# Issuing the small SBUF-to-SBUF transfers from ACT instead of SP, with the order of the work planned anew

## The chip, the cores and the metric

The kernel runs on one core of a Trainium2 chip. The metric is the device time of one execution in microseconds (us). Five engines work in parallel and each takes its own instructions in order: PE (matrix multiply; PEld is its weight load), DVE (vector), ACT (scalar and activation), POOL (GpSimd) and SP, which in this kernel only issues transfers. ACT can issue transfers too. A transfer is issued on the queue of the engine that issues it and then carried by the core's DMA engines.

## What is computed

A linear attention with a decaying state, and behind it two feed-forward networks over the same 3072 tokens (384 columns, 2048 hidden), all in float32:

```python
# B, H, S, D = 4, 8, 768, 48; for each batch and head, over the time t
cur = einsum('bhd,bhe->bhde', u * k_t, v_t)
y_t = einsum('bhd,bhde->bhe', r_t, state + cur)
state = w_t[..., None] * state + einsum('bhd,bhe->bhde', k_t, v_t)
...
x = y.transpose(0, 2, 1, 3).reshape(B * S, H * D)
h = x @ w_in                                   # first network
x = (maximum(h, 0) + alpha * minimum(h, 0)) @ w_out
h = x @ w_in2                                  # second network
out = (h * clip(h + 3, 0, 6) / 6) @ w_out2
```

## The kernel before

**Attention.** The 3072 tokens are cut into 12 thirds of 256 tokens, and the 8 heads into 4 pairs, so there are 48 units (third t, pair pr; number n = 4t + pr). `add_third` loads and weighs the tokens of a third (`load_v`, `load_rk`, `weigh_tokens` L375, `red` L382). `add_unit` does a unit: it loads it (`load`, L412), makes two scans on DVE (L430, L444), scales (L465, DVE or POOL), multiplies on PE (L519, L527, L565, L569, L644, L651, L655), and on ACT it builds diagonals (L502, four instructions), sums a check (L490), copies (L558, L441) and scales states (L589). Its output is split into two float32r parts, hi (ACT, L680) and lo (DVE, L686).

**The transfers of this change.** The columns of the networks' input lie on 128 partitions in three blocks. Pairs 0 to 2 write their parts straight into `XT[j]` (tile names xt, rows 0 to 111 of a block). Pair 3 has no block of its own: its parts go into a staging tile `x3` (name x in the trace, one buffer), and six small transfers (`spread`, L696; 32 KB each, two heads by three blocks) carry them into the free 16-row gaps of the three blocks. So each third has one group of six, 12 groups and 72 transfers in all. A group waits for all hi and lo parts of its third (`before`), and slot 0 of a token block j waits for both groups of its two thirds (`xt_ops`).

**Networks.** The tokens stand in 6 blocks of 512; each network goes over 6 blocks by 16 hidden chunks, which makes 192 slots. A slot (`add_slot`) is nine matmuls into h, `pq` on ACT (L908 or L910), `gate` on DVE (L915 or L919), `ghi` on ACT (L925), `glo` on DVE or POOL (L928), and nine matmuls into acc; each product is three float32r matmuls (L871 to L873). Weights arrive packed (`add_weights`: load L825, then ACT L95, DVE L98 and L103, ACT L839, DVE or POOL L843). Block 0 needs thirds 0 and 1 (units 0 to 7), so the first matmul of slot 0 is the end of a prologue; until then the plan fills PE's gaps with dummy matmuls (`warm`, L772). The units of the other thirds run beside the slots of the first network. The first network's outputs go to memory by SP (`store`, L985) and come back for the second.

**The order.** Nothing is ordered by hand. `Plan.op` records every piece with its possible engines, its modelled duration, a due time in slots and its dependences; `Plan.run` simulates all engines and always takes the earliest piece that can start, the one with the lowest due first. The result is each engine's program order. `URGENCY` shifts due times by kind and stage (below -0.5 slots, to 16, to 80, to 95), and may pin a kind to an engine. SP is modelled as a queue with an issue time (`ISSUE`) and a flight time (`FLIGHT`). `SPARE` is added to the due time of a piece that could run elsewhere when it stands for DVE.

Of the kernel before, what the change touches and what calls it, by code (L numbers as in the profile page):

```python
# [109 lines left out]
def weight_range(nc, v, raw):  # L110
# [8 lines left out]
    "add_range.upper": {3: (2.5, None)},  # L119
    "add_slot.glo": {1: (0, "DVE"), 2: (0, "DVE")},  # L120
    "add_slot.h_": {1: (-3.0, None), 2: (1.0, None), 3: (-1.0, None)},
    "add_third.load_v": {0: (-6.0, None)},
    "add_third.red": {1: (0.5, None), 2: (-1.5, None)},
    "add_unit.add_output.lo_": {0: (1.0, None)},
    "add_unit.diag": {1: (4.0, None)},
    "add_unit.kt": {0: (-3.0, None), 2: (-3.0, None)},
    "add_unit.load": {1: (-1.5, None)},
    "add_unit.recip": {0: (-4.0, None)},
    "add_unit.scan_g": {0: (-4.0, None), 1: (-1.0, None)},
    "add_unit.scan_t": {1: (-1.0, None)},  # L130
    "add_unit.triangle": {0: (2.0, None)},
    "add_weights.hi": {0: (-2.0, None)},
    "add_weights.lo": {1: (-1.5, None)},
    "add_weights.load": {0: (1.0, None), 1: (-2.5, None)},
    "add_weights.rest": {1: (-2.0, None)},
    "join": {0: (-7.0, None)},
    "negate": {0: (-5.0, None)},
    "scale_half": {0: (0, "POOL")},
    "second": {2: (-0.5, None), 3: (2.0, None)},
    "state1": {1: (7.5, None)},  # L140
    "weigh_tokens": {0: (0, "POOL"), 1: (1.0, "DVE"), 2: (0, "DVE")},
# [3 lines left out]
class Plan:  # L145
# [8 lines left out]
    ISSUE, FLIGHT = 0.45, 1.6  # L154
    SPARE = 0
# [15 lines left out]
    def op(self, where, due, fn, after=(), new=(), use=(), pair=False, kind=None):  # L171

        kind = kind or fn.__qualname__.replace("<locals>.", "").split(".", 1)[1]
        if due < self.STAGES[-1]:
# [3 lines left out]
            if engine and len(where) > 1:  # L178
                where = {engine: where[engine]}
        o = {"where": where, "due": due, "fn": fn, "id": len(self.ops), "out": []}  # L180
        o["kind"] = kind
# [17 lines left out]
    def run(self):  # L199
# [6 lines left out]
        free = {e: self.BEGIN[e] for e in ready}  # L206
# [19 lines left out]
        pair = queue = 0.0  # L226
# [8 lines left out]
        while True:  # L235
# [11 lines left out]
            t, _, e, o = best  # L247
# [3 lines left out]
            o["eng"], o["start"], o["end"] = e, t, t + d  # L251
# [3 lines left out]
            if e == "SP":  # L255
                queue = o["end"] = max(t + self.ISSUE + self.FLIGHT, queue) + d
                free[e] = max(t + self.ISSUE, queue - self.FLIGHT - d)
# [14 lines left out]
def fast_path(es, tc, unit, tok, vch, ub, w1, w2, alpha, out, flag, alp, x2d):  # L272
    nc = tc.nc
# [80 lines left out]
    def add_third(t):  # L354
# [7 lines left out]
        v_op[t] = plan.op({"SP": 1.26}, due + 2, load_v, new=[vb]), vb  # L362
        pb = plan.buf("p", 2)
        reds = []
        for c in range(2):
# [22 lines left out]
            o = plan.op({"SP": 1.26}, due + c, load_rk, new=[rb])  # L388
# [9 lines left out]
    def add_unit(n):  # L398
# [15 lines left out]
        o_load = plan.op({"SP": 1.3}, d - 4 if n else -50.0, load, new=[ub_])  # L414
# [247 lines left out]
        def add_output(o_pc, yb2):  # L662
# [30 lines left out]
            if pr == 3:  # L693

                def spread(e, h, i):
                    nc.sync.dma_start(  # L696
                        XT[j][48 + 64 * h : 64 + 64 * h, i, :, cs].bitcast(F32),
                        u["x3"][64 * h + 16 * i : 64 * h + 16 * i + 16].bitcast(F32),
                    )

                before = list(ops)
                for h in range(2):
                    for i in range(NK):
                        ops.append(
                            plan.op(
                                {"SP": 0.48}, d + 2.6, lambda e, h=h, i=i: spread(e, h, i),
                                before, use=[xt_buf[j], x3b],
                                kind="spread",
                            )
                        )  # L710
# [98 lines left out]
    def add_weights(keys, due):  # L809
# [38 lines left out]
        o_l = plan.op({"SP": 1.26 * n}, due - 4, load, new=[wb])  # L848
# [473 lines left out]
```

## Time and profile before

| | us |
|---|---|
| median of 3 runs | 937.88 (932.49 to 1141.69) |
| the profiled execution | 939.31 |
| its span, first to last instruction | 937.5 |
| PE busy | 919.5 (98%) |
| DVE busy | 553.0 (59%) |
| ACT busy | 528.8 (56%) |
| POOL busy | 139.2 (15%) |

The span is taken from the profile; 1.8 us of the execution's time lie around it. A matmul's busy time includes its way through the array and overlaps with its neighbours, so PE can look busy while its matmuls start farther apart than they could. Instructions that issue transfers are not counted as busy time of their engine. Shares over the whole span mix a prologue, a stage in which the first network is fed while its weights are still being unpacked, and a long rest; the views by stretch keep them apart.

### The profile page before, as it was taken

What the parts mean: (1) busy time and instruction counts of PE and PEld (TensorE: products, weight loads), DVE (VectorE), ACT (ScalarE), POOL (GpSimd) and SP (SyncE); (2) the same over time, 40 slices, a digit from 0 to 9 for tenths busy, and PEclk for the clock granted to TensorE, in tenths of its full rate; (3) what the DMA queues carried; (4) which work ended last, traced back from release to release, by engine and by line L of the source; (5) the groups of instructions that cost most, each with busy time, mean ns of one, the idle gap of its engine ahead of it and who ended that gap; (6) DMA issues with size and microseconds to landing.
All of it is one profiled execution on the core that took longest, in us unless ns stands there. A gap on an engine that the chain in (4) does not pass through costs nothing.

```text
span 937.5 us, 13798 instructions
## 1 busy us (share of the span) xinstructions
PE 919.5 (98%) x4999; PEld 753.4 (80%) x4999; DVE 553.0 (59%) x957; ACT 528.8 (56%) x1260; POOL 139.2 (15%) x128
## 2 busy tenths in 40 slices
PE   8999998999999999999999999999999999999997
PEld 6876777888888888888888888888888888888885
DVE  7889996765756665564368987353353443443432
ACT  5988765655655655565357887363353443443331
POOL 7511021100100010010013254020020010200000
PEclk9999999999999999999999999999999999999998
DMA  8798223321322221110045540050140320400001
GB/s 274 227 266 275 68 84 103 110 72 56 119 65 74 98 59 41 56 54 6 8 135 203 176 161 1 0 202 1 48 155 0 135 68 1 168 34 1 35 1 37
DMA packets 36750, 86.20 MB, mean 92 GB/s; under 512 B 5056, under 2 KB 7488, under 8 KB 36672
## 3 DMA queue, kind: packets, MB, share of 16 engines
q1 hardware_dynamic: 36240, 84.44, 28.2%
q8 instruction: 41, 0.67, 0.3%
q10 hardware_dynamic: 432, 0.79, 0.2%
q14 instruction: 37, 0.30, 0.1%
HBM read 73.41 MB, written 9.44 MB: 88 GB/s over the span
## 4 chain that ended last, share of the span: by engine, by line
PE 90%; DVE 3%; DMA 2%; ACT 2%; issue 1%; POOL 0%; SPq 0%; ACTq 0%; DVEq 0%; POOLq 0%
PE acc L871 14%; PE h L871 14%; PE acc L872 14%; PE acc L873 14%; PE h L873 13%; PE h L872 13%; PE A L519 3%; PE y L651 2%; DMA un<-in_unit 2%; PE y L644 2%; PE A L527 1%; DMA rk<-in_tok 1%; DVE tg L444 1%; ACT wa L95 1%; PE y L655 1%
## 5 line engine op out<-in xcount | busy, mean ns | idle before, releaser
L871 PE MATMUL acc<-g,w 128*128 128x512 f32 x576 | 227.8, 396 | 0.0
L872 PE MATMUL acc<-g,w 128*128 128x512 f32 x576 | 225.0, 391 | 2.5 <-DVE g L928 2.5
L873 PE MATMUL acc<-g,w 128*128 128x512 f32 x576 | 224.6, 390 | 0.0
L925 ACT ACTIVATE g<-pg 128x512 fp32r<-128x512 f32 x192 | 120.9, 630 | 135.1 <-PE acc L873 85.8
L928 DVE TENSOR_TENSOR g<-pg,g 128x512 fp32r<-128x512 f32 x162 | 112.6, 696 | 116.5 <-ACT g L925 114.8
L872 PEld LDWEIGHTS acc<-g,w 128*128 128x128 f32 x576 | 108.3, 188 | 25.0 <-DVE g L928 4.0
L919 DVE SCALAR_TENSOR_TENSOR pg<-q,h 128x512 f32<-128x512 f32 x96 | 65.9, 686 | 105.4 <-ACT q L910 105.2
L871 PEld LDWEIGHTS acc<-g,w 128*128 128x128 f32 x576 | 108.8, 189 | 21.9 <-issue 0.4
L873 PEld LDWEIGHTS acc<-g,w 128*128 128x128 f32 x576 | 108.3, 188 | 22.4
L910 ACT ACTIVATE q<-h,three 128x512 f32<-128x512 f32 x96 | 65.6, 684 | 94.9 <-PE h L873 94.8
L871 PE MATMUL h<-xt,w 128*128 128x512 f32 x288 | 113.5, 394 | 2.1 <-DVE pg L915 2.0
L872 PE MATMUL h<-xt,w 128*128 128x512 f32 x288 | 112.6, 391 | 0.0
L873 PE MATMUL h<-xt,w 128*128 128x512 f32 x288 | 112.6, 391 | 0.0
L871 PE MATMUL h<-x,w 128*128 128x512 f32 x288 | 112.0, 389 | 0.0
L872 PE MATMUL h<-x,w 128*128 128x512 f32 x288 | 112.0, 389 | 0.0
L873 PE MATMUL h<-x,w 128*128 128x512 f32 x288 | 112.0, 389 | 0.0
L908 ACT ACTIVATE q<-h,nal 128x512 f32<-128x512 f32 x96 | 65.9, 687 | 72.7 <-PE h L873 67.8
L465 POOL TENSOR_TENSOR kr<-un,tg 112x512 f32<-112x512 f32 (+1 forms) x55 | 55.6, 1012 | 344.9 <-DVE tg L444 266.9
L915 DVE SCALAR_TENSOR_TENSOR pg<-h,q 128x512 f32<-128x512 f32 x96 | 65.7, 686 | 60.0 <-ACT q L908 57.8
L871 PEld LDWEIGHTS h<-xt,w 128*128 128x128 f32 x288 | 54.5, 189 | 15.4 <-issue 2.9
L873 PEld LDWEIGHTS h<-xt,w 128*128 128x128 f32 x288 | 54.4, 189 | 11.5
L872 PEld LDWEIGHTS h<-xt,w 128*128 128x128 f32 x288 | 54.4, 189 | 11.3
(101 smaller groups left out, 1265.9 us busy)
## 6 DMA issues: line engine op xcount, KB each, us to landing
wraw<-in_w SPq DMA_DIRECT2D x64, 384.0 KB, 5.4
un<-in_unit SPq DMA_DIRECT2D x48, 337.3 KB, 3.3
raw<-in_w SPq DMA_DIRECT2D x32, 384.0 KB, 3.7
rk<-in_tok SPq DMA_DIRECT2D x24, 384.0 KB, 4.4
v<-in_vch SPq DMA_DIRECT2D x12, 384.0 KB, 3.4
x2d<-st SPq DMA_DIRECT2D x18, 256.0 KB, 2.1
x2r<-x2d SPq DMA_DIRECT2D x18, 256.0 KB, 4.6
out<-st SPq DMA_DIRECT2D x15, 256.0 KB, 2.2
```

Source lines behind the costliest of these rows:

```text
L465: eng[e].tensor_tensor(out=u["kr"][:, i].rearrange("p a (c s) -> p a c s", c=2), in0=u["in"][:, 0 : 2 * TH].rearrange("p (a c s) -> p a c ...
L519: nc.tensor.matmul(A[h][:, cs], kr[r0 : r0 + D, 0, cs], kr[r0 : r0 + D, 1, cs], start=True, stop=True,)
L644: nc.tensor.matmul(y[:, cs], S[c], u["kr"][:, 1, cs], start=(c == inter[0]), stop=False, skip_group_check=True,)
L871: nc.tensor.matmul(ps, whi, xhi, start=start, stop=False, skip_group_check=True)
L872: nc.tensor.matmul(ps, whi, xlo, start=False, stop=False, skip_group_check=True)
L873: nc.tensor.matmul(ps, wlo, xhi, start=False, stop=stop, skip_group_check=True)
L908: nc.scalar.activation(q, k["h"], AF.Relu, scale=nal[:, f : f + 1])
L910: nc.scalar.activation(q, k["h"], AF.Relu, bias=three)
L915: nc.vector.scalar_tensor_tensor(out=p, in0=k["h"], scalar=0.0, in1=k["q"], op0=ALU.max, op1=ALU.subtract)
L919: nc.vector.scalar_tensor_tensor(out=p, in0=k["q"], scalar=6.0, in1=k["h"], op0=ALU.min, op1=ALU.mult)
L925: nc.scalar.activation(k["g"][:, 0], k["p"], AF.Copy)
L928: eng[e].tensor_tensor(out=k["g"][:, 1], in0=k["p"], in1=k["g"][:, 0].bitcast(F32), op=ALU.subtract)
```

## The change

The six transfers of a group are issued by ACT (`nc.scalar.dma_start`) instead of SP. In the plan each is an ACT piece of 0.45 us with a flight time of 1.9 us before its result counts as there; before, each was an SP piece of 0.48 us. The planned times of the large loads go from 1.26 or 1.30 to 1.35 us, `SPARE` goes from 0 to 1, and the table of urgencies is a new one: 23 kinds before, 38 after. Every engine's order therefore changes, although the pieces of work themselves are the same ones.

```diff
--- before.py
+++ after.py
@@ -116,29 +116,41 @@
 
 
 URGENCY = {
-    "add_range.upper": {3: (2.5, None)},
-    "add_slot.glo": {1: (0, "DVE"), 2: (0, "DVE")},
-    "add_slot.h_": {1: (-3.0, None), 2: (1.0, None), 3: (-1.0, None)},
-    "add_third.load_v": {0: (-6.0, None)},
-    "add_third.red": {1: (0.5, None), 2: (-1.5, None)},
-    "add_unit.add_output.lo_": {0: (1.0, None)},
-    "add_unit.diag": {1: (4.0, None)},
-    "add_unit.kt": {0: (-3.0, None), 2: (-3.0, None)},
-    "add_unit.load": {1: (-1.5, None)},
-    "add_unit.recip": {0: (-4.0, None)},
-    "add_unit.scan_g": {0: (-4.0, None), 1: (-1.0, None)},
-    "add_unit.scan_t": {1: (-1.0, None)},
-    "add_unit.triangle": {0: (2.0, None)},
-    "add_weights.hi": {0: (-2.0, None)},
-    "add_weights.lo": {1: (-1.5, None)},
-    "add_weights.load": {0: (1.0, None), 1: (-2.5, None)},
-    "add_weights.rest": {1: (-2.0, None)},
-    "join": {0: (-7.0, None)},
-    "negate": {0: (-5.0, None)},
-    "scale_half": {0: (0, "POOL")},
-    "second": {2: (-0.5, None), 3: (2.0, None)},
-    "state1": {1: (7.5, None)},
-    "weigh_tokens": {0: (0, "POOL"), 1: (1.0, "DVE"), 2: (0, "DVE")},
+    "add_range.upper": {3: (1.0, None)},
+    "add_slot.gate": {1: (0.5, None)},
+    "add_slot.ghi": {1: (0.5, None)},
+    "add_slot.glo": {1: (0, "DVE"), 2: (-6.0, "DVE")},
+    "add_slot.h_": {1: (-4.5, None), 3: (-3.5, None)},
+    "add_slot.pq": {1: (-1.5, None), 3: (4.5, None)},
+    "add_third.load_rk": {0: (-4.0, None)},
+    "add_third.load_v": {0: (-5.5, None), 1: (2.5, None)},
+    "add_third.red": {0: (4.0, None), 1: (0.5, None)},
+    "add_unit.add_output.hi_": {0: (-3.5, None), 1: (3.0, None)},
+    "add_unit.add_output.lo_": {1: (1.5, None)},
+    "add_unit.check": {0: (0.5, None)},
+    "add_unit.diag": {1: (6.0, None)},
+    "add_unit.keep": {1: (2.5, None)},
+    "add_unit.kt": {0: (-10.0, None), 1: (1.0, None), 2: (-1.5, None)},
+    "add_unit.kv": {0: (-2.5, None), 1: (-3.0, None)},
+    "add_unit.load": {1: (-2.0, None)},
+    "add_unit.pa": {0: (-1.0, None)},
+    "add_unit.recip": {0: (-3.5, None), 2: (3.5, None)},
+    "add_unit.scan_g": {0: (-2.0, None), 1: (-1.0, None)},
+    "add_unit.scan_t": {0: (0.5, None)},
+    "add_unit.triangle": {0: (5.5, None)},
+    "add_weights.hi": {0: (-3.5, None)},
+    "add_weights.lo": {0: (0, "DVE"), 1: (0.5, None), 3: (0, "POOL")},
+    "add_weights.load": {0: (-1.0, None)},
+    "add_weights.rest": {1: (-2.5, None)},
+    "add_x2.lo": {3: (0, "POOL")},
+    "join": {0: (-5.5, None), 1: (1.0, None)},
+    "negate": {0: (-8.5, None)},
+    "output": {1: (5.0, None)},
+    "scale": {2: (0, "DVE")},
+    "scale_half": {0: (-3.0, "POOL")},
+    "second": {1: (2.5, None), 2: (-0.5, None), 3: (4.0, None)},
+    "state1": {1: (3.0, None)},
+    "weigh_tokens": {0: (-1.0, None), 1: (0, "DVE"), 2: (0, "DVE")},
 }
 
 
@@ -151,8 +163,8 @@
     LATENCY = {"PE": 0.26, "DVE": 0.06, "ACT": 0.05, "POOL": 0.08, "SP": 0.0}
     SAME = {"PE": 0.0, "DVE": 0.02, "ACT": 0.02, "POOL": 0.02, "SP": 0.0}
     STAGES = (-0.5, 16, 80, 95)
-    ISSUE, FLIGHT = 0.45, 1.6
-    SPARE = 0
+    FLIGHT = 1.6
+    SPARE = 1
     COLD = 8.0
     BEGIN = {"PE": 1.4, "DVE": 3.1, "ACT": 5.2, "POOL": 3.0, "SP": 0.7}
 
@@ -168,7 +180,8 @@
         line.append(b)
         return b
 
-    def op(self, where, due, fn, after=(), new=(), use=(), pair=False, kind=None):
+    def op(self, where, due, fn, after=(), new=(), use=(), pair=False, kind=None,
+           flight=0.0, issue=0.45):
 
         kind = kind or fn.__qualname__.replace("<locals>.", "").split(".", 1)[1]
         if due < self.STAGES[-1]:
@@ -178,7 +191,7 @@
             if engine and len(where) > 1:
                 where = {engine: where[engine]}
         o = {"where": where, "due": due, "fn": fn, "id": len(self.ops), "out": []}
-        o["kind"] = kind
+        o["kind"], o["flight"], o["issue"] = kind, flight, issue
         o["flex"] = len(where) > 1
         o["pair"] = pair
         full = set(d["id"] for d in after)
@@ -248,13 +261,14 @@
             for x in o["where"]:
                 ready[x].remove(o)
             d = o["where"][e] * (2 if e == "PE" and t < self.COLD else 1)
-            o["eng"], o["start"], o["end"] = e, t, t + d
+            o["eng"], o["start"], o["end"] = e, t, t + d + o["flight"]
             free[e] = t + d - self.TAIL[e]
             if e == "POOL" or (e == "DVE" and o["pair"]):
                 pair = free[e]
             if e == "SP":
-                queue = o["end"] = max(t + self.ISSUE + self.FLIGHT, queue) + d
-                free[e] = max(t + self.ISSUE, queue - self.FLIGHT - d)
+                issue = o["issue"]
+                queue = o["end"] = max(t + issue + self.FLIGHT, queue) + d
+                free[e] = max(t + issue, queue - self.FLIGHT - d)
             if not (o.get("filler") and self.started):
                 seq.append(o)
             else:
@@ -359,7 +373,7 @@
             v_t[t] = ap_.tile([P, 2, DM], F32, tag="v", bufs=2, name=f"v{t}")
             nc.sync.dma_start(v_t[t], vch[t])
 
-        v_op[t] = plan.op({"SP": 1.26}, due + 2, load_v, new=[vb]), vb
+        v_op[t] = plan.op({"SP": 1.35}, due + 2, load_v, new=[vb]), vb
         pb = plan.buf("p", 2)
         reds = []
         for c in range(2):
@@ -385,7 +399,7 @@
                     axis=AX.X, op=ALU.add,
                 )
 
-            o = plan.op({"SP": 1.26}, due + c, load_rk, new=[rb])
+            o = plan.op({"SP": 1.35}, due + c, load_rk, new=[rb])
             for b, after in ((1, []), (None, [o_u])):
                 o = plan.op(
                     {"POOL": 1.0, "DVE": 0.55}, due + 2 + c, lambda e, b=b, m=mul: m(e, b=b),
@@ -411,7 +425,7 @@
             u["in"] = ap_.tile([PR, UW], F32, tag="unit", bufs=3, name=f"un{n}")
             nc.sync.dma_start(u["in"], unit[t, pr])
 
-        o_load = plan.op({"SP": 1.3}, d - 4 if n else -50.0, load, new=[ub_])
+        o_load = plan.op({"SP": 1.35}, d - 4 if n else -50.0, load, new=[ub_])
 
         if early:
             tgb = plan.buf(("q", "pg")[n % 2], 2)
@@ -693,7 +707,7 @@
             if pr == 3:
 
                 def spread(e, h, i):
-                    nc.sync.dma_start(
+                    nc.scalar.dma_start(
                         XT[j][48 + 64 * h : 64 + 64 * h, i, :, cs].bitcast(F32),
                         u["x3"][64 * h + 16 * i : 64 * h + 16 * i + 16].bitcast(F32),
                     )
@@ -703,9 +717,10 @@
                     for i in range(NK):
                         ops.append(
                             plan.op(
-                                {"SP": 0.48}, d + 2.6, lambda e, h=h, i=i: spread(e, h, i),
+                                {"ACT": 0.45}, d + 2.6,
+                                lambda e, h=h, i=i: spread(e, h, i),
                                 before, use=[xt_buf[j], x3b],
-                                kind="spread",
+                                kind="spread", flight=1.9,
                             )
                         )
 
@@ -845,7 +860,7 @@
                 op=ALU.subtract,
             )
 
-        o_l = plan.op({"SP": 1.26 * n}, due - 4, load, new=[wb])
+        o_l = plan.op({"SP": 1.35 * n}, due - 4, load, new=[wb])
         o = plan.op({"ACT": 0.18 + 0.45 * n}, due - 0.2, rest, [o_l], new=[ab, bb], use=[wb])
         for i in (1, 2):
             o = plan.op(
```

## Rows read from the trace of the kernel before

**Rows 1.** The page's head and its part 1: engine busy us (share) xinstructions.

```profile
span 937.5 us, 13798 instructions
PE 919.5 (98%) x4999; PEld 753.4 (80%) x4999; DVE 553.0 (59%) x957; ACT 528.8 (56%) x1260; POOL 139.2 (15%) x128
```

**Rows 2.** Stretches: length, busy (xinstructions) of PE, PEld, DVE, ACT, POOL; clock, DMA share, GB/s.

```profile
20.00:48.00 28.00, 27.55 (x296) 21.78 (x297) 25.17 (x62) 27.24 (x99) 16.88 (x19) 1.00 0.82 244
48.00:56.00 8.00, 6.73 (x70) 5.09 (x69) 5.87 (x12) 6.12 (x22) 1.09 (x1) 1.00 0.74 180
56.00:75.00 19.00, 18.50 (x114) 13.83 (x113) 17.99 (x33) 16.78 (x42) 2.63 (x2) 1.00 1.00 321
75.00:100.00 25.00, 23.34 (x138) 18.16 (x137) 24.21 (x41) 20.77 (x49) 2.67 (x2) 1.00 0.76 242
100.00:140.00 40.00, 39.58 (x212) 30.32 (x211) 38.35 (x65) 28.64 (x64) 6.16 (x5) 1.00 0.19 58
140.00:160.00 20.00, 17.51 (x111) 14.11 (x110) 11.29 (x26) 10.49 (x29) 2.20 (x2) 0.91 0.39 121
160.00:440.00 280.00, 280.00 (x1746) 232.62 (x1745) 169.62 (x330) 170.71 (x490) 31.06 (x28) 1.00 0.22 68
440.00:930.00 490.00, 490.00 (x2180) 405.26 (x2180) 244.90 (x365) 237.73 (x437) 62.91 (x42) 1.00 0.22 73
```

**Rows 3.** Dummy matmuls (L772) alone: length, PE busy, PEld busy, clock, DMA share, GB/s.

```profile
20.00:48.00 28.00, 12.87 (x103) 9.40 (x103) 1.00 0.82 244
```

**Rows 4.** Waits of PE from 56 to 160: us in total, times, longest.

```profile
PE acc L872 <- DVE g L928: 2.5, 1, 2.5
PE h L871 <- DVE pg L915: 2.0, 2, 1.7
```

**Rows 5.** SP's timeline: start us, us from first to last issue, transfers issued.

```profile
29.82 3.92 SPq L696 DMA_DIRECT2D xt<-x  x6
46.88 5.85 SPq L696 DMA_DIRECT2D xt<-x  x6
...
137.48 3.78 SPq L696 DMA_DIRECT2D xt<-x  x6
141.35 0.53 SPq L371 DMA_DIRECT2D rk<-in_tok  x1
142.92 0.45 SPq L371 DMA_DIRECT2D rk<-in_tok  x1
```

**Rows 6.** Tile xt, SP's transfers from 46 to 53: issue ns min/median/max; landing.

```profile
L696 SPq DMA_DIRECT2D xt<-x x6: 585/586/597, 46.9 to 52.1; - x6
DMA to landing us min/median/max: 3.0/6.2/7.4
```

**Rows 7.** The same view from 137 to 142; transfers issued from 42 to 47, median landing.

```profile
DMA to landing us min/median/max: 1.9/2.0/2.0
...
wraw<-in_w SPq DMA_DIRECT2D x2, 384.0 KB, 9.1
```

**Rows 8.** Timeline of PEld at slot 0, and of PE at its longest wait.

```profile
55.95 0.19 PEld L871 LDWEIGHTS h<-xt,w 128*128 128x128 f32 x1
...
150.99 0.75 PE L872 MATMUL acc<-g,w 128*128 128x512 f32 x1 [2.49 <-DVE g L928]
```

**Rows 9.** DVE's timeline around that wait; in brackets idle time and what ended it.

```profile
138.40 0.54 DVE L382 TENSOR_REDUCE p<-rk 128x8 f32<-128x384 f32 x1
...
145.45 0.56 DVE L375 TENSOR_TENSOR rk<-rk 128x384 f32<-128x384 f32 x1 [3.20 <-DMA rk<-in_tok]
...
149.78 0.56 DVE L375 TENSOR_TENSOR rk<-rk 128x384 f32<-128x384 f32 x1 [2.58 <-DMA rk<-in_tok]
150.25 0.68 DVE L928 TENSOR_TENSOR g<-pg,g 128x512 fp32r<-128x512 f32 x1
```

**Rows 10.** Lines L985 and L696: issue ns min/median/max; SP's own waits ahead of a group.

```profile
L985 ACTq DMA_DIRECT2D out<-st x3: 339/381/1700, 929.9 to 931.5; - x3
L696 SPq EVENT_SEMAPHORE  x12: 17/1134/15858, 27.9 to 422.7; - x12
```

## The prediction

> **What bounds the kernel.** I read the page's engine shares first. PE is busy 98% of a span of 937.5 us, DVE 59%, ACT 56% [rows 1]. That says little here, since PE also counts dummy matmuls as busy. The view by stretch shows where time can be had at all. From 160 to 440 and from 440 to 930 PE is busy all 280.00 and all 490.00 us at full clock, with DVE and ACT well below it [rows 2]. In those 770 us nothing this change does off PE can shorten the run; it can only lengthen it.
>
> So the change plays in the first 160 us, which have three parts. From 20 to 48 ACT is busy 27.24 of 28 us and DVE 25.17, while PE fills 12.87 us with dummies [rows 2, 3]: ACT sets when slot 0 can begin, with DVE close behind. From 56 to 140 DVE is full, 17.99 of 19, 24.21 of 25 and 38.35 of 40 us, while ACT has 16.78, 20.77 and 28.64 [rows 2]; there DVE feeds PE. From 140 to 160 everything thins out: DVE 11.29 and PE 17.51 of 20 us, mean clock 0.91 [rows 2].
>
> The waits of PE say what is lost at sharp places after slot 0: one wait of 2.5 us for `glo` (L928) and two of together 2.0 us for `gate` (L915) [rows 4]. SP's timeline shows where the moved transfers stand in this. A group occupies SP for 3.8 to 5.85 us [rows 5], one issue alone taking 0.59 us [rows 6], so about 0.64 us from issue to issue.
>
> **Part 1: six issues on ACT, twelve times.** I take the same 0.64 us on ACT, 3.84 us a group. The lower bound is the only transfers that ACT issues now, 0.34 us each at the least [rows 10], 6 x 0.34 = 2.0 us. The upper is SP's slowest group, 5.85 us [rows 5]. In the whole kernel it is 12 x 3.84 = 46 us of ACT, but only the first four groups lie before 160. What they cost depends on the cover:
>
> - Third 0, near 30 us: ACT is 97% busy from 20 to 48, so the 3.84 us push back what follows. There is some cover, because ACT also does work there for units beyond the eight that slot 0 needs, and the new plan may put that behind. Bounds 0 and +5.9; I take +3.8, because the row of that stretch shows no idle time to speak of.
> - Third 1, near 47 us: the group is itself the last input of slot 0, so its issuing is on the path before and after. What it holds back on ACT is other units' work; 8 - 6.12 = 1.9 us were idle there [rows 2]. 0 here, its landing is part 2.
> - Thirds 2 and 3, near 82 and 137 us: from 75 to 140 ACT has 25 - 20.77 + 40 - 28.64 = 15.6 us idle, twice what two groups take (7.7 us), and DVE is the limit. 0; if that cover is gone, because a group sits ahead of a `ghi` that PE waits for, up to +3.8 once.
> - The other eight, after 160: ACT's 170.71 of 280 us become at most 201. The plan has a slot's second matmuls due 2.5 slots behind its `ghi`, and PE never waits in that stretch now. 0, with +4 as the upper bound for one group that overruns this slack.
>
> **Part 2: the last input of slot 0.** Third 1's group is issued from 46.88 on [rows 5], its last transfer at 52.1; the shortest landing in that group is 3.0 us and the longest 7.4 [rows 6], against 1.9 to 2.0 us on a quiet queue [rows 7]. In front of it stand large loads on the same queue; the weights issued just before take 9.1 us to land [rows 7]. So the group is down at about 52.1 + 3.0 = 55.1, and slot 0's first weight load follows at 55.95 [rows 8]. On ACT's own queue nothing stands ahead: 46.88 + 5 x 0.64 + 2.0 = 52.1. Gain 3.0 us; bounds 0 (it still waits among the loads) and 3.0, since the visit of another unit ahead of slot 0 on PE would then become the last. I take -3.0, the value of the quiet row, because it is what stands on the same queue that differs between the two.
>
> **Part 3: SP freed.** At 137.48 a group holds SP for 3.78 us, and the load of the tokens of a third (`load_rk`) follows at 141.35, a second at 142.92 [rows 5]. DVE, in order, stands 3.20 and then 2.58 us for these two loads; behind the second stands the `glo` at 150.25 [rows 9], for which PE waits 2.49 us at 150.99 [rows 8]. This is the largest wait of PE. After it the clock is low: 20 us at 0.91 [rows 2] cost 20 x 0.09 = 1.8 us. Without the group ahead, the first load can go once its buffer is free, after the reduction at 138.40 plus 0.54 [rows 9], at 139.0, so 2.4 us sooner. The second is bound by its buffer rather than by the group and gains little by itself; its stall goes only if the new order does not put a ready `glo` behind a late load again. Bounds 0 and -(2.5 + 1.8) = -4.3. I take -4.3, because both ingredients are changed: the group is off SP, and the planned load is longer (1.35 for 1.26), so the plan reckons later with its arrival.
>
> SP's own semaphore waits ahead of a group (median 1.1, up to 15.9 us [rows 10]) also held back loads behind it. In the DVE-bound stretch earlier weights buy nothing: 0.
>
> **Part 4: the new order elsewhere.** Urgencies, `SPARE` and load times reorder every engine. The trace before can't show that order. It adds no work, so its gain is bounded by what DVE leaves idle between 20 and 140: 120 - (25.17 + 5.87 + 17.99 + 24.21 + 38.35) = 8.4 us [rows 2]. Its loss has no such bound; the nearest size is PE's present waits, 4.5 us [rows 4], doubled, +4.5. I take 0.
>
> **The sum.** +3.8 - 3.0 - 4.3 + 0 = -3.5 us. Span 937.5 - 3.5 = 934.0; with the 1.8 us around it, 935.8 against the profiled 939.31. That execution lies 1.4 us above the median, so the forecast on the median's scale is 934.4, rounded to 934.5.
>
> **Rivals.**
>
> *ACT becomes the bound (slower).* A group is in order on ACT, so ACT also waits there for the last lo part on DVE, and everything behind it waits too: `ghi`, `pq`, the copies for PE. SP showed such waits, 1.1 us in the median. A group then costs 3.84 + 1.1 = 4.9 us. Thirds 0 and 1 in full, less the 1.9 us idle, are 7.9; a third 2 that falls into 56 to 75, where ACT has 19 - 16.78 = 2.2 us left, adds 2.7. Without the gains of parts 2 and 3 that is +10.6, on the median's scale 948.5. It decides from the point where a group stands ahead of a piece that slot 0 or a matmul needs. For it speaks the 97%; against it that the plan counts 0.45 us a transfer on ACT and can put deferrable checks behind.
>
> *Nothing lands sooner.* The transfers are carried by the same DMA engines, and those are 74 to 100% busy from 48 to 75 [rows 2]. Then part 2 is 0 and SP's time is the only thing saved: +3.8 - 4.3 = -0.5, median's scale 937.4. The Trainium skill, page "DMA: Bandwidth & Descriptors", section "Issuing engines are not separate DMA queues", states this rule: transfers from several engines run on the same DMA engines, and issuing elsewhere saves only the sequencer's time; by it the sum would be -0.5 instead of -3.5. The same page, section "Queues, rings and completion order", says that a DMA engine takes turns between queues packet by packet, which would let the small ones pass; no row here shows two busy queues at once.
>
> *The stall reappears.* The new order again parks a ready `glo` behind a late load: +3.8 - 3.0 = +0.8, 938.7.
>
> *The order packs DVE tighter.* The 8.4 us of part 4 come in full: 926.0.
>
> **Chances.** Forecast (931 to 938) 0.40; tighter packing (923 to 931) 0.19; nothing sooner or the stall back (936 to 941) 0.22; ACT the bound (942 to 952) 0.19. The likeliest case's own range is 931 to 938. To leave out no more than 2 in 10, the range takes in most of the packing case and the lower half of the slow one: 925 to 947. The band of 2%, about what a measurement of this kernel can tell from no change, is 919 to 957. Faster would need more than all bounds of gain together (8.4 + 3.0 + 4.3 = 15.7 us, against 18.8): 0.03. Slower needs the ACT case plus a loss in the order: 0.04. Within: 0.93.
>
> **What would show it.** In the changed profile: groups on ACT at 0.64 us from issue to issue and landing in 2 us (parts 1, 2); slot 0's first weight load near 56.8 (+3.8 - 3.0); no wait of DVE over 1 us for token loads near 140 to 150, and clock 1.00 there (part 3); PE full from 160 on. The forecast is wrong if slot 0 moves past 60, if PE waits for `ghi` or `pq` behind a group, or if PE shows waits after 160.

## The result

The changed kernel takes 942.88 us (median of 12 runs, 941.16 to 946.87), the kernel before 937.03 (12 runs); the ratio is 1.0081, 95% interval 1.0064 to 1.0098. So it is 0.8% slower: inside the band of 2% and inside the range on record, but on the other side of the forecast of 934.5. The ratio compares the runs of the two kernels and is not the quotient of the two medians, which is 1.0062; kernels are compared by such ratios below. The profiled execution took 941.16 us, the lowest of its runs, while that of before lay above its median. The two traces show where the time goes, but their spans differ by only 1.8 us, so sizes are taken from the timed comparisons.

The page of the changed kernel, its head, part 1 and two lines of part 3 (queue: packets, MB, share of the DMA engines):

```profile
span 939.3 us, 13713 instructions
PE 923.7 (98%) x4996; PEld 755.9 (80%) x4996; DVE 568.3 (61%) x987; ACT 526.4 (56%) x1258; POOL 109.6 (12%) x100
q1 hardware_dynamic: 32784, 82.07, 27.5%
q10 hardware_dynamic: 3888, 3.15, 1.4%
```

ACT is no busier than before [rows 1], although it now issues the 72 transfers: issuing does not count as busy. The 3.15 MB on q10 show the change itself (72 x 32 KB and three stores of 256 KB).

The stretches of the changed kernel (length; busy of PE, PEld, DVE, ACT, POOL; clock, DMA share, GB/s), to be laid beside [rows 2]:

```profile
20.00:48.00 28.00, 26.22 (x249) 20.02 (x247) 22.08 (x53) 20.98 (x73) 11.60 (x15) 0.88 0.82 241
48.00:56.00 8.00, 6.79 (x65) 5.27 (x63) 4.38 (x8) 2.79 (x9) 1.35 (x2) 1.00 0.90 280
56.00:75.00 19.00, 17.37 (x87) 12.97 (x88) 15.17 (x27) 15.42 (x42) 2.56 (x2) 0.82 0.63 204
75.00:100.00 25.00, 24.10 (x150) 18.22 (x149) 24.32 (x41) 21.29 (x54) 3.77 (x3) 1.00 0.93 288
140.00:160.00 20.00, 20.00 (x116) 16.43 (x113) 18.45 (x39) 14.21 (x40) 2.28 (x2) 1.00 0.38 113
160.00:440.00 280.00, 280.00 (x1751) 232.60 (x1750) 185.94 (x360) 170.15 (x488) 0.00 (x0) 1.00 0.24 70
```

From 20 to 56 ACT's busy time falls by 9.6 us (27.24 + 6.12 to 20.98 + 2.79) and DVE's by 4.6. So in the tightest stretch of the kernel ACT does less work. From 140 to 160, on the other hand, PE is full and the clock 1.00: the dip of before is gone.

Why ACT stands there shows in its timeline (start us, us; in brackets idle time of ACT's compute and what ended it; ACTq rows are issues, the length from the first to the last):

```profile
28.83 0.72 ACTq L710 DMA_DIRECT2D xt<-x  x1
...
31.68 2.47 ACTq L710 DMA_DIRECT2D xt<-x  x3
34.19 1.38 ACT L603 ACTIVATE sbd<-Y,tg 48x48 f32<-48x48 f32 x4 [3.48 <-DMA wraw<-in_w]
...
50.21 4.59 ACTq L710 DMA_DIRECT2D xt<-x  x5
54.85 0.84 ACT L854 ACTIVATE w<-wb 128x768 fp32r<-128x768 f32 x1 [4.38 <-DMA xt<-x]
```

SP's timeline at the same time, six weight loads in each of the two bursts:

```profile
28.13 8.86 SPq L840 DMA_DIRECT2D wraw<-in_w  x6
...
48.66 7.89 SPq L840 DMA_DIRECT2D wraw<-in_w  x6
```

And PE (its waits over the whole span, then two rows of its timeline at slot 0):

```profile
PE h L886 <- DMA xt<-x: 2.8, 1, 2.8
...
PE y L658 <- ACT sbd L603: 1.8, 2, 1.5
```

```profile
57.63 0.77 PE L886 MATMUL h<-xt,w 128*128 128x512 f32 x1 [2.84 <-DMA xt<-x]
58.20 0.63 PE L887 MATMUL h<-xt,w 128*128 128x512 f32 x1
```

The two groups of the prologue stretch over 5.3 us of ACT (28.83 to 34.15) and 6.8 us (48.03 to 54.80), with 3.48 and 4.38 us of idle compute in them. In the second, some 1.6 us lie between the first issue and the next, in which ACT has compute pieces of its own. Slot 0 waits for the second group. During that wait the granted clock falls to the lower of its two levels (0.50, 1.2 instead of 2.4 GHz; 56.56 to 63.39): matmuls take 0.63 us after it, and a mean clock of 0.82 over 19 us is 19 x 0.18 = 3.4 us lost, where before had 1.00. The first stretch has as long a fall (0.88 over 28 us, 36.08 to 42.91), at a time when no slot has begun; what that one costs, no run separates.

How far the kernels are at the same slot, worked out from the traces (start of the first matmul of h of a slot, us from the span's start; the runs with an e are explained below):

```
slot              0       1       8      12      16      24      95
before        55.97   58.13   93.30  117.95  141.79  186.08  525.40
after         57.63   62.12  100.79  124.64  146.71  186.66  527.34
e1            51.49   57.81   96.06  119.95  142.09  181.99  522.67
e2            59.46   63.45   98.54  123.81  149.13  189.90  529.22
e4            53.48   55.64   93.26  113.88  136.25  176.18  516.85
e12           53.95   56.12   94.32  117.06  140.90  180.86  520.24
```

The changed kernel loses 7.5 us up to slot 8 and wins 6.1 back between slots 12 and 24, where before had its stall. But e1, the same plan with the transfers on SP, wins the same 6.1 there: 62.0 us from slot 12 to slot 24 in both, 68.1 in the kernel before.

### The profile page after: what moved, and what is told of

It reads as the page before. It is cut to its first block, busy times and chain, and to the rows that moved or that the text cites. A ratio compares the mean times of both kernels' runs of the same rounds, so it can differ in the third digit from the quotient of the medians.

```text
span 939.3 us, 13713 instructions
## 1 busy us (share of the span) xinstructions
PE 923.7 (98%) x4996; PEld 755.9 (80%) x4996; DVE 568.3 (61%) x987; ACT 526.4 (56%) x1258; POOL 109.6 (12%) x100
## 3 DMA queue, kind: packets, MB, share of 16 engines
q10 hardware_dynamic: 3888, 3.15, 1.4%
## 4 chain that ended last, share of the span: by engine, by line
PE 91%; DVE 3%; ACT 2%; DMA 2%; issue 1%; SPq 0%; ACTq 0%; POOL 0%; DVEq 0%; POOLq 0%
PE h L886 14%; PE acc L886 13%; PE h L887 13%; PE h L888 13%; PE acc L887 13%; PE acc L888 13%; PE A L533 3%; PE y L665 2%; PE y L658 2%; PE A L541 1%; PE warm L787 1%; DMA u_sb<-in_ub 1%; DVE wb L98 1%; DMA xt<-x 1%; DMA wraw<-in_w 1%
## 5 line engine op out<-in xcount | busy, mean ns | idle before, releaser
L888 PEld LDWEIGHTS h<-x,w 128*128 128x128 f32 x288 | 54.0, 188 | 11.3
```

The costliest lines, as they stand in the source:

```text
L888: nc.tensor.matmul(ps, wlo, xhi, start=False, stop=stop, skip_group_check=True)
```

## The experiments

Two theories stood at the start. Q: the queue is the cause; on ACT the groups cost the prologue more than SP's freed time gives. P: the plan is the cause; the new table is worse, whichever queue carries the groups. Four kernels cross queue and plan.

**e1: the new plan, transfers issued from SP.**

```diff
-                    nc.scalar.dma_start(
+                    nc.sync.dma_start(
                         XT[j][48 + 64 * h : 64 + 64 * h, i, :, cs].bitcast(F32),
```

> The changed kernel with one line back: the 72 small transfers are issued from SP again, each at the place in SP's program that the new plan gives it; every other engine keeps the new order instruction for instruction. Theory Q (the queue: on ACT a group is held up by the large loads in flight, ACT stands 3.5 and 4.4 us idle in the two groups of the prologue, and slot 0 comes late): most of the loss comes back, 936 to 939 us, no idle stretch of ACT over 2 us between 28 and 55. Theory P (the plan: the new table of urgencies itself is worse, whichever queue carries the group): stays at 941 to 945 us, slot 0 no earlier than 57.

Measured: 936.18 us beside 935.49 for the kernel before, ratio 1.0004 (0.9985 to 1.0023). Everything lost comes back with one word, while all other engines keep their order. Three stretches of e1:

```profile
20.00:48.00 28.00, 27.19 (x292) 21.26 (x291) 26.17 (x56) 23.77 (x85) 13.36 (x16) 1.00 0.89 270
48.00:56.00 8.00, 5.82 (x43) 4.50 (x40) 5.68 (x12) 4.91 (x13) 2.42 (x2) 0.90 0.90 293
140.00:160.00 20.00, 20.00 (x130) 16.64 (x130) 17.97 (x38) 14.15 (x41) 1.39 (x1) 1.00 0.38 120
```

ACT works 4.9 us more and DVE 5.4 us more before 56 than with the groups on ACT, and slot 0 begins at 51.49 instead of 57.63. The last row matters for part 3 of the prediction: the stall of before is gone with the transfers on SP as well.

**e2: the old plan, transfers issued from ACT.**

```diff
-                    nc.sync.dma_start(
+                    nc.scalar.dma_start(
                         XT[j][48 + 64 * h : 64 + 64 * h, i, :, cs].bitcast(F32),
```

> The kernel before with one line changed: the 72 small transfers are issued from ACT, at the place that the old plan gives them; every other order stays. Theory Q: slower by the price of two groups in a full ACT, +4 to +10 us, 941 to 947 us, ACT's issuing of the first two groups over 4.5 us each and landing over 4 us. Theory P: within 2 us of the kernel before, 935 to 939 us. The part of my forecast on SP's freed time would show as DVE's waits for token loads near 142 to 150 going from 5.8 us to under 3 us.

Measured: 942.68 us, ratio 1.0081 (1.0053 to 1.0108), as theory Q expected. The line alone costs as much as the whole change. PE's longest total wait from 20 to 170, and DVE's wait for token loads from 135 to 170:

```profile
PE y L644 <- ACT sbd L589: 4.5, 2, 4.0
```

```profile
DVE rk L375 <- DMA rk<-in_tok: 2.3, 1, 2.3
```

PE waits up to 4.0 us for a state that ACT could not scale behind the group. DVE's waits for token loads fall from 5.8 [rows 9] to 2.3 us: SP's freed time does its part (66.1 us from slot 12 to 24 instead of 68.1), and it isn't enough.

**e3: transfers planned and issued on ACT, but with the old table, load times and `SPARE`** (against the changed kernel; `URGENCY` is that of the kernel before).

```diff
-    SPARE = 1
+    SPARE = 0
...
-         v_op[t] = plan.op({"SP": 1.35}, due + 2, load_v, new=[vb]), vb
+         v_op[t] = plan.op({"SP": 1.26}, due + 2, load_v, new=[vb]), vb
...
-        o_l = plan.op({"SP": 1.35 * n}, due - 4, load, new=[wb])
+        o_l = plan.op({"SP": 1.26 * n}, due - 4, load, new=[wb])
```

> Planned anew with the transfers as ACT pieces (0.45 us, flight 1.9 us) as in the changed kernel, but with the old table of urgencies, the old load times and SPARE 0. Theory Q: slower than before by more than the changed kernel or about equal to it, 941 to 950 us, since the old table was not chosen for it. Theory P: faster than the changed kernel, 934 to 940 us.

Measured: 948.30 us, ratio 1.0151 (1.0122 to 1.0180), in the range of theory Q.

**e4: the new table, load times and `SPARE`, transfers planned and issued on SP.**

```diff
-                    nc.scalar.dma_start(
+                    nc.sync.dma_start(
...
-                                {"ACT": 0.45}, d + 2.6,
+                                {"SP": 0.48}, d + 2.6,
...
-                                kind="spread", flight=1.9,
+                                kind="spread",
```

> The new table, SPARE 1 and load times 1.35, with the transfers planned and issued on SP as before (0.48 us). Theory Q: 935 to 940 us, slot 0 before 57. Theory P: 941 us or more.

Measured: 930.70 us, ratio 0.9949 (0.9930 to 0.9969), faster than either theory expected and the fastest kernel of this study. With e3 and the two kernels this makes a square: on SP 1 (old table, load times and `SPARE`) and 0.9949 (new), on ACT 1.0151 and 1.0081. With the order planned for each queue the move to ACT costs 1.3 to 1.5%; with the order kept, e1 and e2 had 0.8%. The new table with its load times and `SPARE` gains 0.5 to 0.7% on either queue. Theory P falls. Stretches of e4, and all that PE waits for from 20 to 170:

```profile
20.00:48.00 28.00, 27.49 (x293) 21.23 (x291) 26.31 (x59) 25.78 (x95) 15.98 (x18) 1.00 0.87 251
48.00:56.00 8.00, 8.00 (x67) 6.38 (x66) 7.49 (x14) 7.73 (x21) 2.37 (x2) 1.00 0.80 217
75.00:100.00 25.00, 25.00 (x158) 19.07 (x156) 23.91 (x43) 20.25 (x50) 4.25 (x3) 1.00 0.71 236
```

```profile
PE A L579 <- ACT kT L572: 0.2, 1, 0.2
PE y L658 <- DVE xt L700: 0.2, 1, 0.2
PE h L886 <- DVE pg L930: 0.2, 1, 0.2
```

From 48 to 56 ACT is busy 7.73 of 8 us, where the changed kernel has 2.79.

**e5 and e6: where on the way is the price paid?** Both keep the changed kernel's plan. e5 issues thirds 0 and 1 from SP, the rest from ACT (below); e6 has the two names swapped.

```diff
-                    nc.scalar.dma_start(
+                    (nc.sync if t < 2 else nc.scalar).dma_start(
```

> The changed kernel and its plan, but the groups of thirds 0 and 1, the two of the prologue, are issued from SP; the other ten stay on ACT. If the price is paid in the prologue, where the large loads are in flight and slot 0 waits: like the kernel with all of them on SP under this plan, 935 to 938 us. If each group on ACT costs its share wherever it lies (12 groups, 6.7 us): only a sixth comes back, 941 to 943 us.

> The mirror image: only the groups of thirds 0 and 1 on ACT, the other ten on SP, the plan of the changed kernel. Price in the prologue: 941 to 944 us, as the changed kernel. Share for each group: 936 to 939 us.

Measured: e5 935.99 us, ratio 1.0003 (0.9989 to 1.0018); e6 943.32 us, ratio 1.0075 (1.0052 to 1.0099). Under this plan the two groups of the prologue are the whole price. The ten later ones are free within some 0.2%.

**e7: issuing without anybody waiting.** The transfers that count are on SP; ACT issues a copy of each into a spare tensor in memory. It carries twelve more groups than the others.

```diff
-                    nc.scalar.dma_start(
+                    nc.sync.dma_start(
                         XT[j][48 + 64 * h : 64 + 64 * h, i, :, cs].bitcast(F32),
                         u["x3"][64 * h + 16 * i : 64 * h + 16 * i + 16].bitcast(F32),
                     )
+                    nc.scalar.dma_start(
+                        spare[t, h, i],
+                        u["x3"][64 * h + 16 * i : 64 * h + 16 * i + 16].bitcast(F32),
+                    )
```

> The transfers that count are all on SP, at the new plan's places; at the places where the changed kernel issues them on ACT, ACT issues as many transfers of the same source and size into a spare memory tensor that nothing reads. So ACT pays for the issuing, and no matmul waits for what it issues. If ACT's held sequencer is the price: 940 to 944 us and idle stretches of ACT over 2 us near 30 and 50. If the late landing on a shared set of DMA engines is the price: 935 to 938 us, as with SP alone.

Measured: 939.10 us, ratio 1.0037 (1.0021 to 1.0054), between the two expectations. ACT's timeline:

```profile
31.59 3.04 ACTq L715 DMA_DIRECT2D spare<-x  x4
34.68 1.38 ACT L604 ACTIVATE sbd<-Y,tg 48x48 f32<-48x48 f32 x4 [4.11 <-DMA spare<-x]
...
54.20 0.84 ACT L859 ACTIVATE w<-wb 128x768 fp32r<-128x768 f32 x1 [3.04 <-DMA spare<-x]
```

PE's longest wait from 20 to 170:

```profile
PE h L891 <- DMA xt<-x: 2.9, 1, 2.9
```

ACT stands idle nearly as long as in the changed kernel (4.11 and 3.04 us beside 3.48 and 4.38), although nothing reads what it issues, and by the ratios that costs 0.33% over e1, of the 0.77% between e1 and the changed kernel. This is no clean share: a copy takes 0.43 us to issue in the median instead of 0.61, the added transfers also hold SP's (how, is told under e10), and slot 0 still waits 2.9 us for its input. That ACT's lost time is part of the price is shown; that the rest is slot 0's wait for the landing, with the clock after it, is argued from the changed kernel's trace and not measured alone.

**e8: the new table planned anew with thirds 0 and 1 on SP, the others on ACT** (against the changed kernel).

```diff
-                    nc.scalar.dma_start(
+                    (nc.sync if e == "SP" else nc.scalar).dma_start(
...
-                                {"ACT": 0.45}, d + 2.6,
+                                {"SP": 0.48} if t < 2 else {"ACT": 0.64}, d + 2.6,
...
-                                kind="spread", flight=1.9,
+                                kind="spread", flight=0.0 if t < 2 else 1.4,
```

> The new table planned anew with thirds 0 and 1 on SP and thirds 2 to 11 on ACT (0.64 us each, flight 1.4 us). If ACT is harmless once the loads of the prologue are through: 928 to 932 us, level with the version that plans all on SP (930.7 us) or better, since SP is freed near 86 and 131. If any group in the stretch where DVE feeds PE costs: 933 to 938 us.

Measured: 936.25 us, ratio 0.9997 (0.9982 to 1.0013), so by the ratios 0.5% behind e4 and in the range of the second expectation. One stretch of e8:

```profile
75.00:100.00 25.00, 21.73 (x131) 15.73 (x130) 21.13 (x38) 16.08 (x36) 2.67 (x2) 0.97 0.78 256
```

The plan now put third 2's group beside a run of weight loads, from 86.09 on. The group stretches over 6.5 us of ACT again, and DVE, which feeds PE there, does 2.8 us less than in e4. This speaks against the prologue as such, and for a group beside a run of loads while ACT's work is wanted; the whole order differs from e4's too.

**e9: the plan told what a transfer really costs** (issue and landing, 1.0 and 4.5 us in the prologue, 0.64 and 1.4 us later).

```diff
-                                {"ACT": 0.45}, d + 2.6,
+                                {"ACT": 1.0 if t < 2 else 0.64}, d + 2.6,
...
-                                kind="spread", flight=1.9,
+                                kind="spread", flight=4.5 if t < 2 else 1.4,
```

> The changed kernel planned with what was measured: a transfer of thirds 0 and 1 costs ACT 1.0 us and is in flight for 4.5 us, of the others 0.64 and 1.4 us. If the loss is a matter of wrong costs in the plan (0.45 and 1.9 us): 934 to 938 us. If ACT simply has no room for two groups in the prologue: 941 to 946 us.

Measured: 939.69 us, ratio 1.0032 (1.0014 to 1.0050), between the two expectations. More than half of the loss (0.81% to 0.32%) was a matter of costs in the plan. Where the rest lies isn't shown: the profiled execution, 936.76 us, is one of the fastest of runs that go from 936.29 to 942.83, and its trace has no wait of PE over 0.6 us from 20 to 170.

**e10 and e11: do the bytes of the loads hold ACT?** Both load only half the columns of the first network's weights; the other half is set to zero and so left out of the product. e10 has the changed kernel's queue, e11 that of e1.

```diff
-                nc.sync.dma_start(k["raw"][:, i], (w1, w2)[m][f, part])
+                cols = slice(0, DM if m else DM // 2)
+                nc.sync.dma_start(k["raw"][:, i, cols], (w1, w2)[m][f, part, :, cols])
+                if m == 0:
+                    nc.gpsimd.memset(k["raw"][:, i, DM // 2 :].bitcast(I32), 0)
```

> The changed kernel with the weight loads of the first network cut to half their columns (the rest is set to zero on POOL, so half of these weights is left out); transfers on ACT as in the changed kernel. If the large loads in flight are what holds ACT's issuing: a group of the prologue takes 3.8 to 4.5 us on ACT instead of 5.3 and 6.8 and lands in 2 to 3 us, and the kernel is at most 3 us slower than its partner with the transfers on SP. If issuing beside SP costs by itself: still 5 us and more a group, and 5 to 8 us slower than its partner.

> The partner: the same halved weight loads and the same plan, transfers issued from SP. Loads in flight as the cause: 930 to 936 us, and within 3 us of the partner on ACT. Issuing beside SP as the cause: 5 to 8 us under the partner on ACT.

Measured: e10 942.67 us (ratio 1.0066, 1.0044 to 1.0088), e11 932.71 us (0.9958, 0.9944 to 0.9972). With half the bytes the gap grew to 10 us, beyond both expectations. ACT's and SP's timelines of e10:

```profile
31.66 5.58 ACTq L710 DMA_DIRECT2D xt<-x  x4
37.28 1.38 ACT L603 ACTIVATE sbd<-Y,tg 48x48 f32<-48x48 f32 x4 [6.74 <-DMA xt<-x]
```

```profile
27.25 8.50 SPq L841 DMA_DIRECT2D wraw<-in_w  x6
```

ACT is held even longer, and SP's six half loads take 8.50 us to issue, nearly the 8.86 of the whole ones. Nor do they land sooner: the first three take 7.2 to 8.2 us from issue to landing, those of the changed kernel 5.4 to 7.1. So theory Q had the wrong reason: not the bytes.

What holds an issue stands in the traces. Each transfer raises a semaphore (a counter that instructions can wait for) when it lands. The program has eight semaphores for this, SP's and ACT's transfers take them in turn, and an issue waits until the transfer that had its semaphore before has landed. The source of the kernel sets none of this itself. Worked out from the changed kernel's trace, every issue from 28.13 to 35.46:

```
issue starts   queue  transfer   on the way before it (SP + ACT)   semaphore, its last transfer landed   lands
28.13          SP     wraw       3 + 0                             102, 24.74                            33.53
28.60          SP     wraw       4 + 0                             105, 27.23                            35.10
28.83          ACT    xt         5 + 0                             101, 22.78                            35.45
29.59          ACT    xt         5 + 1                             103, 26.12                            36.17
29.62          SP     wraw       4 + 2                             107, 29.61                            36.69
30.28          ACT    xt         5 + 2                             106, 28.11                            36.89
31.68          ACT    xt         4 + 3                             108, 31.65                            37.09
32.79          ACT    xt         3 + 4                             110, 32.77                            37.29
33.55          ACT    xt         2 + 5                             102, 33.53                            37.48
35.46          SP     wraw       1 + 5                             101, 35.45                            38.37
```

The issues at 29.62, from 31.68 to 33.55 and at 35.46 start 0.02 us after the landing of the transfer that had their semaphore before. In the fourteen traces of this study (4384 transfers) no transfer starts before that landing, and 110 start within 0.03 us of it. Eight semaphores also keep the number on the way at eight or less, but the number is not what holds: in 33 of the 110 cases fewer than eight were out. The last row is one. At 35.10 a landing left seven on the way, and SP's load still waited for 35.45, when the ACT transfer of 28.83, which had semaphore 101, landed. So a transfer that moves to ACT brings along a wait for the eighth transfer before it, in the prologue nearly always a load of SP, and ACT's compute stands behind it. In the two groups of the prologue such waits make up 1.5 us each.

Two more things can be read here. The landings come in the order of the issues, across the two queues: in the changed kernel only 5 of 139 pairs on different queues, issued over 0.1 us apart while the first was still on the way, landed the other way round. And the first transfer of the first group lands 6.6 us after its issue although nothing stood ahead on its own queue.

**e12: where e4's gain comes from.** e4 with the old table: load times 1.35 and `SPARE` 1 stay. Three of its rows:

```diff
-    "add_unit.kt": {0: (-10.0, None), 1: (1.0, None), 2: (-1.5, None)},
...
-    "negate": {0: (-8.5, None)},
-    "output": {1: (5.0, None)},
...
+    "add_unit.kt": {0: (-3.0, None), 2: (-3.0, None)},
...
+    "negate": {0: (-5.0, None)},
```

> Transfers on SP, load times of 1.35 us and SPARE 1, but the old table of urgencies. If the gain of the version with the new table on SP (930.7 us) comes from load times and SPARE: 929 to 933 us. If it comes from the table: 935 to 942 us.

Measured: 932.84 us beside 936.70, ratio 0.9973 (0.9955 to 0.9991). The time lies in the first expectation's range, but the kernel before was slower beside it too. By the ratios load times and `SPARE` give 0.27% of the 0.51% by which e4 is faster; the table seems to give the rest, but the two intervals overlap.

## Why the prediction was wrong

**What bounds the kernel: right.** The first 160 us decided it, ACT sets the start of slot 0, and PE is full for 280.00 of 280 us from 160 on, as [rows 2] had it.

**Part 1, six issues on ACT: the price of an issue was right, that of a group was not.** An issue takes 0.61 us and a group on a quiet system 3.84 us, as forecast (141.96 to 145.80). In the prologue the groups stretched over 5.3 and 6.8 us of ACT instead of 3.8, 1.5 us of each in waits for SP's loads to land. The row that showed this was in hand: in SP's group of 5.85 us [rows 5] the issues at 49.00, 50.12 and 52.14 started 0.02 us after the landing of the load that had their semaphore. I used it as an upper bound only, and for third 1 I set 0, because ACT had idle time beside it. That step failed worst: 4.38 us of ACT's compute stood still, and the 1.9 us of cover was no match.

**Part 2, the last input of slot 0: wrong, with its sign.** The step was "on ACT's own queue nothing stands ahead". The next rows are landing times of the small transfers (us from issue to landing, least, median, most). First the first group: in the kernel before, in e1 and in the changed kernel.

```profile
DMA to landing us min/median/max: 1.9/2.0/2.2
```

```profile
DMA to landing us min/median/max: 2.9/3.8/4.3
```

```profile
DMA to landing us min/median/max: 3.9/6.0/6.6
```

Then the changed kernel's second group, and its fourth, which has no loads beside it:

```profile
DMA to landing us min/median/max: 4.3/5.5/6.5
```

```profile
DMA to landing us min/median/max: 2.0/2.0/2.0
```

A queue of its own did not bring the 2 us of the quiet row. The last transfer of the second group landed 4.3 us after its issue, where 3.0 was the row of before [rows 6] and 2.0 the forecast. The first group, which had a quiet landing before, lost it, and under one and the same plan it landed later from ACT (6.0 us) than from SP (3.8). With SP no longer held by the group, loads were issued beside it, where before they had to wait behind it. Slot 0's first weight load came at 57.60 against the 56.8 of the sum, which agrees by accident: the new order by itself brought slot 0 forward by 4.5 us (e1, 51.49 against 55.97), and the queue set it back by 6.1.

**Part 3, SP freed: place and size right, the reason wrong.** No wait of DVE for a token load is left from 135 to 160, PE has 20.00 of 20 us at clock 1.00, and 6.1 us come back between slots 12 and 24; 4.3 were forecast. But e1, where SP isn't freed, has all of this too. It is the new order that removes the stall: load times and `SPARE` alone, with the transfers on SP, bring 4.3 us between these slots (e12), the queue alone under the old order 2.0 (e2). The prediction had named the longer planned load as its second ingredient; that the term came out is luck as far as the queue goes.

**Part 4, the new order: 0 was taken, about -5 us is what it gives when it is planned for SP** (e4), inside the bound of 8.4. Planned for ACT and run on SP it gives nothing in sum (e1): it wins before slot 0 and behind slot 12, and it loses between slots 0 and 8 (44.6 us there against 37.3). The new table has 35 kinds, not 38.

**The sum.** Of +3.8 - 3.0 - 4.3 the -4.3 came, by the order; the -3.0 did not come, and the cost was too small. The move of the queue alone costs 0.8% under the new plan (1.0081 against e1's 1.0004) and under the old one (e2's 1.0081), some 7 us, where the forecast's own terms for it came to -3.5. None of the signs that were to show the forecast wrong appeared: slot 0 stayed before 60, PE waited neither for `ghi` nor for `pq`, and it had no waits after 160.

**The rivals.** "ACT becomes the bound" named the place and the side, with a chance of 0.19, and its 948.5 was too high because the gain that part 3 counted on came all the same. Its mechanism was only half right: ACT waited for loads of SP to land, more than for DVE's last part. "Nothing lands sooner" was right about part 2. The Trainium skill, page "DMA: Bandwidth & Descriptors", section "Issuing engines are not separate DMA queues", says that moving transfers to another engine saves the issuing time alone, and this trace agrees in that nothing was gained by the landing (6.0 us from ACT against 3.8 from SP in the first group). The turns between queues that its section "Queues, rings and completion order" describes did not let the small transfers pass here (134 of 139 pairs landed in the order of their issue).

What stays open: how the loss divides between ACT's issuing, its waits and the late landing, and what the move would cost if each queue had semaphores of its own. No run here changed the semaphores, and none changed the number of loads on the way without changing the order.

## What to carry to other kernels

Moving a transfer to another engine's queue moves its issuing time into that engine's instruction stream, and with it any wait that stands ahead of the issue, a wait for a semaphore that another engine's load still holds included. Before such a move, look in the trace for back-to-back issues that start farther apart than their neighbours, and for the landing that lets each one go. There the new owner will stand still, and if it is a compute engine near 97% busy, that is lost. Small transfers that a critical piece waits for landed fast where no loads were issued just ahead of them (2.0 us), and a queue of their own did not bring that.

A gain that comes out as forecast still needs its cause tested: here one run with the old queue and the new order showed that it came from the order.

## What the runs showed of the hardware

- No transfer started before the one that had its semaphore before it had landed (14 traces, 4384 transfers, eight semaphores for SP and ACT together), and 110 started within 0.03 us of that landing. This is a wait of the program; since it alone keeps the number on the way at eight or less, the runs can't tell whether the chip has a limit of its own. A held issue on ACT stops ACT's compute instructions behind it (3.48 and 4.38 us idle).
- Transfers of the two queues landed nearly always in the order in which they were issued (134 of 139 pairs in the changed kernel).
- Halving the bytes of the loads left the time that six of them take to issue beside a group nearly as it was (8.50 against 8.86 us).
- Issuing one of these small transfers (32 KB) takes 0.59 us on SP and 0.61 us on ACT in the median, while large loads of 384 KB take as little as 0.33 us to issue.
- During PE's wait of 2.84 us the granted clock fell to 0.50, and its matmuls took 0.63 us instead of 0.39 us, for about 5.7 us (57.6 to 63.3).
